# Gated linear attention with a gated convolution layer: the first chunks' convolution in turned 32x32 diagonal blocks on TensorE, and a new order

## The chip, the cores and the metric

One Trainium2 chip, one of its eight cores. The engines of the core work side by side, each through its own queue in order: TensorE (PE) multiplies matrices, VectorE (DVE) and ScalarE (ACT) work element by element, GpSimd (POOL) too, and SyncE (SP) issues the transfers between HBM and the chip's memory, SBUF. TensorE writes its results to PSUM, eight banks of 512 float32 columns on 128 partitions. The metric is the time of one execution in microseconds (us); lower is better.

## The reference

Four sequences of 768 steps, eight heads of 48. The first part is a recurrence with a decayed state, the second a causal convolution of five taps per channel, which gates a projection.

```
f = 1 / (1 + exp(-f_logit))
for t in range(S):                                   # S = 768
    state = f[t] (row by row) * state + outer(k[t], v[t])
    y[t] = q[t] @ state
x = y with the heads side by side                    # [4, 768, 384]
gate_pre[t] = sum over j in 0..4 of conv_w[j] * x[t - 4 + j]
gate = 1 / (1 + exp(-gate_pre))
out = (gate * (x @ w_val)) @ w_out
```

## The kernel before

The 768 steps are six chunks of 128 (c), each with four sequences (b); a sequence's eight heads lie in pairs (p), 48 rows each, on partitions 0 to 47 and 64 to 111. For a chunk, ScalarE forms -log f in two passes (`pexp`, `pln`), VectorE adds it up along time (`scan`), and ScalarE turns the sums into two factors (`exp1`, `exp2`) with which VectorE multiplies q and k (`pmulq`, `pmulk`). TensorE then computes `scores` = k q for a sequence into `aps`, VectorE masks them with a triangle (`mask`, one instruction of 128x1024 into `asb`, one of two buffers); TensorE transposes k (`ktrans` into `kps`, evacuated by `kevac`), applies scores and state to v and q (`apply`, into one of two `xps`, four column tiles of 32 side by side), and forms the chunk's part of the state (`dstate` into `dps`). `stadd` (VectorE) and `stmul` (POOL, line 355) bring the state up to date, `stcopy` (ScalarE) lays it out for the next chunk. `xevac` (ScalarE) copies the result of `apply` into `xf`, channels on partitions: 384 channels are three blocks m of 128; `halo` (POOL, line 328) copies the last four columns of a chunk ahead of the next.

The second layer works on a whole chunk, 512 columns (four sequences by 128 steps); the last chunk is cut into two halves, called 5 and 6. `msplit` (ScalarE) and `mlow` (VectorE) split x into two parts of fewer bits, `xH` and `xL`. The convolution is `mlast` on ScalarE (the newest tap, a multiplication) and four `mconv` on VectorE for each block m, `gt` = `xf` shifted times a weight per partition, plus `gt`; `gate` is the sigmoid. `mval` is a product of nine matmuls (three blocks, three pairs of parts), `mmul` multiplies it by the gate, `mhigh` and `mrest` split the result, and `mout` is nine matmuls more; `mstore` copies to SBUF and sends. The weights come as 64-bit numbers; `weight` (lines 211 to 243) turns them into float32 in eight steps, of which POOL does the first and the last, ScalarE two, VectorE four.

What an engine does and in what order stands in `PROGRAM`, a list of pieces such as `mconv 1 0 2` (chunk 1, block 0, tap 2). `Ordered` binds the instructions of PE, VectorE and ScalarE to that order; POOL and SP take theirs as the scheduler sets it. Tiles in PSUM are fixed: `aps` (two banks), two `xps`, `kps`, `dps` and two `mps` for the projections. `busy` issues matmuls on zeros (26 in the first 18 us). A copy of the computation for extreme inputs (`general`) stands behind a branch and isn't taken here.

Of the kernel before, what the change touches and what calls it, by code (L numbers as in the profile page):

```python
# [37 lines left out]
loadk 1 0; pmulk 0 0; pexp 0 2; loadq 1 0; pmulq 0 0; ktrans 0 0; loadv 0 2; scan 0 1; pln 0 2; scores 0 0; exp2 0 1;  # L40
scan 0 2; wload 1; exp1 0 1; busy 4; kevac 0 0; pmulq 0 1; exp2 0 2; dstate 0 0; pmulk 0 1; busy 4; exp1 0 2;
mask 0 0; loadv 1 0; ktrans 0 1; loadf 2 0; okc 0; kevac 0 1; pmulq 0 2; scores 0 1; pexp 1 0; weight 0; pmulk 0 2;
apply 0 0; pln 1 0; mask 0 1; loadf 3 0; loadk 2 0; dstate 0 1; wload 2; ktrans 0 2; scores 0 2; kevac 0 2; scan 1 0;
xevac 0 0; stadd 0 0; exp2 1 0; ktrans 0 3; mask 0 2; apply 0 1; kevac 0 3; pmulk 1 0; scores 0 3; stcopy 0 0;
scan 1 1; xevac 0 1; exp1 1 0; ktrans 1 0; loadk 2 1; mask 0 3; apply 0 2; exp2 1 1; loadq 2 0; pmulq 1 0; exp1 1 1;
apply 0 3; loadv 2 0; weight 1; weight 0; xevac 0 2; weight 0; pmulq 1 1; scores 1 0; xevac 0 3; weight 1; halo 1;
msplit 0; weight 1; loadq 2 1; weight 1; dstate 0 2; mask 1 0; dstate 0 3; kevac 1 0; ktrans 1 1; weight 0; stadd 0 1;
scores 1 1; kevac 1 1; pmulk 1 1; loadv 2 1; pexp 2 0; weight 0; weight 1; dstate 1 1; weight 1; apply 1 0; okc 1;
mask 1 1; weight 1; loadf 4 0; pln 2 0; weight 1; mlow 0; weight 3; ktrans 1 2; loadk 3 0; scores 1 2; xevac 1 0;
stcopy 0 1; scan 2 0; apply 1 1; mask 1 2; exp2 2 0; exp1 2 0; weight 0; scan 2 1; weight 2; scores 1 3; loadq 3 0;  # L50
mlast 0 0; pmulk 2 0; xevac 1 1; weight 2; exp2 2 1; mconv 0 0 0; dstate 1 0; mask 1 3; apply 1 2; loadv 3 0;
kevac 1 2; exp1 2 1; pmulq 2 0; ktrans 1 3; pmulq 2 1; scores 2 0; loadk 3 1; kevac 1 3; xevac 1 2; mconv 0 0 1;
weight 3; mlast 0 1; stadd 1 0; ktrans 2 0; weight 2; mlast 0 2; dstate 1 2; stmul 1 0; weight 3; dstate 1 3;
weight 3; stcopy 1 0; apply 1 3; weight 2; mask 2 0; kevac 2 0; stadd 1 1; okc 2; scores 2 1; loadv 3 1; weight 2;
xevac 1 3; stmul 1 1; pmulk 2 1; loadq 3 1; stcopy 1 1; mconv 0 2 0; ktrans 2 1; pexp 3 0; dstate 2 0; loadk 4 0;
weight 2; apply 2 0; weight 3; mask 2 1; kevac 2 1; loadf 5 0; weight 2; mconv 0 1 0; pln 3 0; dstate 2 1; weight 2;
mconv 0 1 1; ktrans 2 2; apply 2 1; weight 4; mconv 0 1 2; kevac 2 2; stadd 2 0; weight 3; stmul 2 0; mconv 0 0 2;
weight 3; dstate 2 2; loadq 4 0; stcopy 2 0; scan 3 0; weight 3; scores 2 2; loadv 4 0; weight 5; mconv 0 0 3;
exp2 3 0; mval 0 0; mconv 0 1 3; gate 0 0; mconv 0 2 1; mconv 0 2 2; mval 0 1; mask 2 2; exp1 3 0; mmul 0 0;
ktrans 2 3; scan 3 1; mval 0 2; weight 4; weight 4; exp2 3 1; mconv 0 2 3; exp1 3 1; scores 2 3; pmulq 3 0; halo 2;  # L60
xevac 2 0; pmulk 3 0; kevac 2 3; gate 0 2; apply 2 2; loadk 4 1; mask 2 3; pmulq 3 1; xevac 2 1; dstate 2 3; weight 5;
gate 0 1; scores 3 0; weight 5; xevac 2 2; stadd 2 1; weight 5; stmul 2 1; weight 4; ktrans 3 0; weight 4; apply 2 3;
pexp 4 0; mask 3 0; weight 4; pmulk 3 1; scores 3 1; loadv 4 1; loadq 4 1; mmul 0 1; kevac 3 0; mmul 0 2; weight 4;
ktrans 3 1; pln 4 0; weight 5; weight 4; dstate 3 0; loadk 5 0; weight 5; apply 3 0; mask 3 1; weight 6; weight 5;
scan 4 0; weight 5; weight 6; scores 3 2; kevac 3 1; weight 6; xevac 2 3; exp2 4 0; weight 6; weight 6; apply 3 1;
exp1 4 0; weight 6; mask 3 2; mhigh 0 1; mhigh 0 0; mrest 0 1; dstate 3 1; loadq 5 0; weight 6; mrest 0 0; scores 3 3;
mhigh 0 2; loadv 5 0; weight 6; mlast 1 0; mrest 0 2; mlast 1 1; pmulk 4 0; mout 0 1; msplit 1; mconv 1 0 0;
mconv 1 0 1; mlast 1 2; mout 0 0; mconv 1 1 0; mstore 0 1; mconv 1 0 2; mconv 1 1 1; mout 0 2; mstore 0 0; mlow 1;
ktrans 3 2; mconv 1 0 3; mval 1 0; kevac 3 2; mconv 1 1 2; mstore 0 2; mconv 1 2 0; gate 1 0; stadd 3 0; ktrans 3 3;
mconv 1 1 3; stmul 3 0; mval 1 2; loadk 5 1; mconv 1 2 1; gate 1 1; mmul 1 0; stcopy 3 0; mconv 1 2 2; mval 1 1;  # L70
mhigh 1 0; mconv 1 2 3; kevac 3 3; stcopy 2 1; scan 4 1; halo 3; xevac 3 0; dstate 3 3; xevac 3 1; pmulq 4 0;
dstate 3 2; gate 1 2; apply 3 2; exp2 4 1; stadd 3 1; okc 3; mask 3 3; stmul 3 1; ktrans 4 0; mmul 1 2; pexp 5 0;
scores 4 0; mrest 1 0; mmul 1 1; pmulk 4 1; apply 3 3; mhigh 1 1; mhigh 1 2; mask 4 0; kevac 4 0; exp1 4 1;
dstate 4 0; mrest 1 1; loadq 5 1; mlast 2 0; scores 4 1; loadv 5 1; mrest 1 2; stcopy 3 1; mconv 2 0 0; pln 5 0;
mconv 2 0 1; mout 1 1; mask 4 1; msplit 2; scan 5 1; ktrans 4 1; mout 1 2; xevac 3 2; pmulq 4 1; exp2 5 1; mlow 2;
exp1 5 1; scores 4 2; kevac 4 1; mstore 1 1; pmulq 5 1; mlast 2 2; ktrans 4 2; mout 1 0; kevac 4 2; mconv 2 2 0;
mlast 2 1; mconv 2 0 2; xevac 3 3; scan 5 0; apply 4 0; mconv 2 0 3; exp2 5 0; mconv 2 1 0; exp1 5 0; dstate 4 1;
mconv 2 1 1; apply 4 1; gate 2 0; mask 4 2; pmulk 5 1; mstore 1 0; scores 4 3; mconv 2 2 1; mconv 2 2 2; mval 2 0;
mask 4 3; mstore 1 2; mconv 2 1 2; mval 2 1; mconv 2 2 3; mmul 2 0; pmulq 5 0; mhigh 2 0; ktrans 4 3; mval 2 2;
pmulk 5 0; kevac 4 3; gate 2 2; okc 4; stadd 4 0; scores 5 0; stmul 4 0; msplit 3; mmul 2 2; mconv 2 1 3; mrest 2 0;  # L80
mhigh 2 2; halo 4; dstate 4 2; xevac 4 0; dstate 4 3; mrest 2 2; stcopy 4 0; apply 4 2; stadd 4 1; xevac 4 1;
stmul 4 1; gate 2 1; mlast 3 2; mmul 2 1; apply 4 3; xevac 4 2; mask 5 0; mlast 3 0; mconv 3 0 0; apply 5 0;
mconv 3 0 1; xevac 4 3; mhigh 2 1; mconv 3 0 2; stcopy 4 1; mlow 3; scores 5 1; okc 5; mrest 2 1; mval 3 1; mlast 3 1;
mask 5 1; mconv 3 0 3; mval 3 0; mconv 3 2 0; gate 3 0; mconv 3 2 1; mconv 3 2 2; scores 5 2; mmul 3 0; mconv 3 2 3;
mval 3 2; mask 5 2; mconv 3 1 0; scores 5 3; msplit 4; mconv 3 1 1; mconv 3 1 2; gate 3 2; apply 5 1; mconv 3 1 3;
mmul 3 2; gate 3 1; halo 5; mmul 3 1; mout 2 0; xevac 5 1; mask 5 3; xevac 5 0; mlast 5 2; mlow 4; msplit 5; mout 2 2;
mlast 5 1; mstore 2 0; mlast 5 0; mconv 5 1 0; mlow 5; mout 2 1; mconv 5 0 0; mconv 5 0 1; mconv 5 2 0; mconv 5 0 2;
apply 5 3; mconv 5 1 1; mhigh 3 1; mconv 5 2 1; mhigh 3 2; mhigh 3 0; mrest 3 2; mconv 5 0 3; apply 5 2; mlast 4 2;
mrest 3 1; mstore 2 1; mconv 5 2 2; xevac 5 3; mrest 3 0; mconv 5 1 2; mlast 4 0; mval 4 0; mconv 5 1 3; mconv 4 0 0;
gate 5 1; xevac 5 2; mconv 4 0 1; mstore 2 2; mval 5 0; mlast 6 1; mconv 4 0 2; mlast 6 2; msplit 6; mout 3 0;  # L90
# [561 lines left out]
```

## Time and profile before

| | |
|---|---|
| time, median of 3 runs | 218.72 us (218.57 to 218.86) |
| the profiled execution | 220.51 us, its span 218.8 us |
| PE busy, share of the span | 184.7 us, 84% |
| VectorE | 192.4 us, 88% |
| ScalarE | 144.3 us, 66% |
| POOL | 34.0 us, 16% |
| mean granted clock of TensorE | 0.921 |
| moved by DMA | 31.9 MB |

The span runs from the first to the last instruction. Matmuls are pipelined, so PE's busy time holds time in which one of them drains while nothing else can start. Granted clock: 1 is 2.4 GHz, 0.5 is 1.2 GHz. An instruction's duration overlaps the next one's start on VectorE by some 0.08 us. An engine that is idle costs nothing by itself; what counts is which engine the others wait for, stretch by stretch.

### The profile page before, as it was taken

What the parts mean: (1) busy time and instruction counts of PE and PEld (TensorE: products, weight loads), DVE (VectorE), ACT (ScalarE), POOL (GpSimd) and SP (SyncE); (2) the same over time, 40 slices, a digit from 0 to 9 for tenths busy, and PEclk for the clock granted to TensorE, in tenths of its full rate; (3) what the DMA queues carried; (4) which work ended last, traced back from release to release, by engine and by line L of the source; (5) the groups of instructions that cost most, each with busy time, mean ns of one, the idle gap of its engine ahead of it and who ended that gap; (6) DMA issues with size and microseconds to landing.
All of it is one profiled execution on the core that took longest, in us unless ns stands there. A gap on an engine that the chain in (4) does not pass through costs nothing.

```text
span 218.8 us, 5685 instructions
## 1 busy us (share of the span) xinstructions
PE 184.7 (84%) x2438; PEld 148.4 (68%) x2438; DVE 192.4 (88%) x251; ACT 144.3 (66%) x226; POOL 34.0 (16%) x37
## 2 busy tenths in 40 slices
PE   7599599857997478768999888999989999999970
PEld 2257468755876366557787767877868788889870
DVE  5396998999999999999979999999799999997700
ACT  5767678777492989768289988737823769453530
POOL 4001001500437522312035000002100000000000
PEclk9959958988699999995899996999999999999996
DMA  6999999964079021722141321020000102210231
GB/s 165 368 414 425 414 419 421 415 231 163 23 269 325 36 69 39 271 85 98 61 132 50 100 82 48 3 99 3 3 3 0 36 15 99 96 48 27 96 145 38
DMA packets 10976, 31.91 MB, mean 146 GB/s; under 512 B 1344, under 2 KB 2368, under 8 KB 10688
## 3 DMA queue, kind: packets, MB, share of 16 engines
q1 hardware_dynamic: 10944, 31.48, 38.7%
q8 instruction: 21, 0.34, 0.6%
q14 instruction: 11, 0.09, 0.1%
HBM read 26.75 MB, written 4.72 MB: 144 GB/s over the span
## 4 chain that ended last, share of the span: by engine, by line
DVE 41%; PE 33%; ACT 11%; issue 5%; DMA 5%; SPq 1%; DVEq 0%; ACTq 0%
PE mps L113 21%; DVE gt L113 10%; DVE e L113 10%; DVE asb L113 7%; ACT e L113 5%; PE aps L113 5%; DMA kb<-in_k 5%; PE xps L113 3%; DVE kb L113 3%; DVE qb L113 3%; DVE ca L113 2%; PE kps L113 2%; DVE cb L113 2%; PE dps L113 2%; DVE xL L113 2%
## 5 line engine op out<-in xcount | busy, mean ns | idle before, releaser
L113 ACT ACTIVATE e<-e 112x1024 f32<-112x1024 f32 (+3 forms) x40 | 40.0, 1004 | 18.1 <-DVE e L113 17.7
L113 DVE SCALAR_TENSOR_TENSOR gt<-xf,cws,gt 128x512 f32<-128x512 f32 x60 | 45.4, 775 | 0.6
L113 PE MATMUL aps<-qb,kb 48*128 48x128 f32 x384 | 30.4, 302 | 13.0 <-DVE asb L113 10.7
L113 PE MATMUL xps<-asb,vb 128*32 128x128 f32 x768 | 38.3, 295 | 0.9 <-DVE asb L113 0.9
L113 PEld LDWEIGHTS aps<-qb,kb 48*128 48x128 f32 x384 | 25.6, 204 | 18.8 <-DVE asb L113 12.8
L113 PEld LDWEIGHTS xps<-asb,vb 128*32 128x32 f32 x768 | 32.8, 118 | 2.4 <-ACT e L113 0.9
L113 PE MATMUL mps<-rg,woH 128*128 128x512 f32 (+1 forms) x102 | 33.5, 414 | 0.3 <-DVE gt L113 0.3
L113 PE MATMUL xps<-qb,st 112*32 112x128 f32 x480 | 31.5, 286 | 1.8 <-ACT xf L113 1.8
L113 DVE TENSOR_TENSOR_SCAN e<-keep,e 112x1024 f32<-112x1024 bf16 (+1 forms) x13 | 29.1, 2247 | 3.1 <-ACT e L113 3.0
L113 DVE TENSOR_TENSOR asb<-aps,tri 128x1024 f32<-128x1024 f32 x24 | 29.1, 1214 | 0.2 <-PE aps L113 0.2
L113 PEld LDWEIGHTS xps<-qb,st 112*32 112x32 f32 x480 | 22.5, 114 | 4.1 <-ACT xf L113 2.1
L113 PEld LDWEIGHTS mps<-rg,woH 128*128 128x128 f32 x102 | 19.8, 206 | 4.7 <-DVE gt L113 0.6
L113 PE MATMUL mps<-xH,wvH 128*128 128x512 f32 x45 | 18.6, 414 | 3.1 <-DVE gt L113 2.9
L113 PE MATMUL mps<-rg,woL 128*128 128x512 f32 (+1 forms) x51 | 20.6, 404 | 0.0
L355 POOL TENSOR_TENSOR ss<-u,e 112x384 f32<-112x384 f32 x8 | 9.4, 1173 | 61.7 <-DVE u L113 57.8
L113 PE MATMUL mps<-xL,wvH 128*128 128x512 f32 x45 | 17.9, 397 | 0.9 <-DVE xL L113 0.9
L113 DVE TENSOR_TENSOR kb<-kb,e 112x1024 f32<-112x1024 f32 (+1 forms) x13 | 15.4, 1185 | 3.5 <-DMA kb<-in_k 3.5
L113 PE MATMUL mps<-xH,wvL 128*128 128x512 f32 x45 | 17.8, 395 | 0.0
L113 PE MATMUL kps<-ident,kb 112*128 112x112 f32 x80 | 13.3, 295 | 3.4 <-DVE kb L113 2.3
L113 DVE TENSOR_TENSOR qb<-qb,e 112x1024 f32<-112x1024 f32 (+1 forms) x13 | 14.6, 1130 | 0.0
L113 ACT COPY osb<-mps 128x512 f32<-128x512 f32 x15 | 8.6, 584 | 8.8 <-PE mps L113 6.5
L113 ACT CAST rg<-gt 128x512 fp32r<-128x512 f32 x15 | 9.0, 616 | 8.1 <-DVE gt L113 5.5
(107 smaller groups left out, 308.5 us busy)
## 6 DMA issues: line engine op xcount, KB each, us to landing
...
```

The source lines that it names most:

```text
L113: ins = emit(*a, **kw)
L355: nc.gpsimd.tensor_tensor(out=ss[:, HS[h]], in0=U[h][:], in1=decay(c, h), op=ALU.mult)
```

## The change

**Convolution of chunks 0 and 1.** For these chunks `mlast` and `mconv` are replaced by `pconv`. The five weights of a channel stand on the diagonals of 32x32 blocks (`diag`, formed once by VectorE from `cws` and `eye`), and one tap is twelve float32 matmuls of 32 rows, 32 columns of weights and 512 moving columns: row group i and block m write to partitions 32 x ((i + m) mod 4) of the bank of m. So the twelve use twelve different tiles of the array, and in a group of 32 partitions the three blocks write three different banks; but block m comes out turned by 32 x m partitions. The gate is read from PSUM by `gate`. Since the gate is turned, the projection must be too: `wv` comes with 480 columns instead of 384 in a row block, from which `mval` takes turned columns, and `mout` uses copies of `wo` with turned rows (`woHr`, `woLr`), made by eight transfers on SP (`wturn`). Chunks 2 to 6 keep `mlast` and `mconv`.

**POOL** sets constants only. `stmul` and the last step of the weights (`wlow`) go to VectorE, `halo` to ScalarE; the first step of the weights is another one (`wabs` on ScalarE, a limit on VectorE in `wbits`).

**PSUM** is one tile, `bank`, of eight banks, and each piece is given a bank by the number behind it in `PROGRAM`. Scores take any two neighbours.

**Order.** `PROGRAM` is a new list, SP is bound to it as well, copies and transfers of the output are two pieces (`ocopy`, `ostore`), and `busy` is not in it. f is turned into the decay in place (`fb` instead of `e`), chunk 0 goes in four parts of 512 columns, `keep` is float32, and the test for extreme inputs is made of three pieces at the end.

```
-    def mgate(w, m):
-        act(SIG, w["gt"][:, m], w["gt"][:, m], AF.Sigmoid)
...
+    def pconv(w, j, zs):
+
+        for i in range(4):
+            for m in range(NM):
+                r, o = slice(32 * i, 32 * i + 32), 32 * ((i + m) % 4)
+                PE.matmul(bank[o : o + 32, zs[m], : w["n"]], diag[r, m * KT + j], w["xf"][r, m, w["b"], j : j + C],
+                          start=(j == 0), stop=(j == HALO), tile_position=(32 * i, o))
+
+    def mgate(w, m, z):
+        g = w["gt"][:, m]
+        act(SIG, g, g if z is None else bank[:, z, : w["n"]].rearrange("p (b t) -> p b t", t=C), AF.Sigmoid)
...
+    def wturn(m):
+
+        for s, d in ((woH, woHr), (woL, woLr)):
+            for to, of in ((slice(32 * m, 128), slice(0, 128 - 32 * m)), (slice(0, 32 * m), slice(128 - 32 * m, 128))):
+                SP.dma_start(d[to, m - 1].bitcast(F32), s[of, m].bitcast(F32))
+
+    def wdiag():
+        DVE.tensor_tensor(out=diag[:], in0=cws[:].unsqueeze(2).to_broadcast([128, NM * KT, 32]),
+                          in1=eye[:].unsqueeze(1).to_broadcast([128, NM * KT, 32]), op=ALU.mult)
...
+    def wbits(n):
+        ca, cb = wab(n)
+        hi, bi = wdst(n)[:, :, 1], cb.bitcast(I32)
+        DVE.tensor_scalar(out=cb, in0=cb, scalar1=low, scalar2=big, op0=ALU.max, op1=ALU.min)
+        DVE.tensor_scalar(out=bi, in0=bi, scalar1=3, scalar2=0x3FFFFFF8, op0=ALU.logical_shift_left, op1=ALU.bitwise_and)
+        DVE.scalar_tensor_tensor(out=bi, in0=hi, scalar=-(1 << 30), in1=bi, op0=ALU.bitwise_and, op1=ALU.bitwise_or)
+        x = cws[:] if n == 0 else ca
+        DVE.scalar_tensor_tensor(out=x.bitcast(I32), in0=wdst(n)[:, :, 0], scalar=29, in1=bi,
+                                 op0=ALU.logical_shift_right, op1=ALU.bitwise_or)
...
     def stmul(c, h):
-        nc.gpsimd.tensor_tensor(out=ss[:, HS[h]], in0=U[h][:], in1=decay(c, h), op=ALU.mult)
+        DVE.tensor_tensor(out=ss[:, HS[h]], in0=U[h][:], in1=decay(c, h), op=ALU.mult)
...
+    def mval(w, m, po):
+        at = WCOLS[m] + (0 if w["turn"] else 32 * m)
+        mm3(po, lambda kk: wvH[:, kk, at : at + 128], lambda kk: wvL[:, kk, at : at + 128], w["xH"], w["xL"])
...
+        def of(t, tr):
+            return lambda kk: (tr[:, kk - 1, cols] if w["turn"] and kk else t[:, kk, cols])
```

How the order moves, at three places. PE in chunk 1, before: scores (`aps`), transposition (`kps`) and state parts (`dps`) of chunk 1 stand behind the state parts of chunk 0, and `apply` (`xps`) follows.

```order
L113 MATMUL aps<-qb_65,kb_67 128x128 x8
L113 MATMUL dps<-vb_70,ksb_86 48x48 x8
L113 MATMUL dps<-vb_70,ksb_87 48x48 x8
L113 MATMUL kps<-ident,kb_67 128x112 x4
L113 MATMUL aps<-qb_65,kb_67 128x128 x8
L113 MATMUL dps<-vb_71,ksb_87 48x48 x8
L113 MATMUL xps_105<-qb_65,st 32x128 x4
```

The same place now; all results go to `bank`.

```order
L126 MATMUL bank<-ident,kb_67 128x112 x8
L126 MATMUL bank<-xf_88,diag 32x512 x12
L126 MATMUL bank<-qb_65,kb_67 128x128 x16
L126 MATMUL bank<-xf_88,diag 32x512 x48
L126 MATMUL bank<-vb_71,ksb_86 64x48
```

The first tap of chunk 0's convolution comes ahead of two sequences' scores, the other four, 48 matmuls, ahead of the first state part of chunk 1.

VectorE around the second half of chunk 2's scans, before: masks (`asb`), convolution of chunk 0 (`gt<-xf,cws,gt`), weights (`ca`, `cb`), state (`u`).

```order
L113 TENSOR_TENSOR asb_85<-aps,tri 128x1024
L113 SCALAR_TENSOR_TENSOR gt<-xf_90,cws,gt 128x512 x3
L113 TENSOR_TENSOR u_88<-ss,dps 112x384
L113 SCALAR_TENSOR_TENSOR ca_102<-raww_95,cb_103 128x384
L113 SCALAR_TENSOR_TENSOR gt<-xf_90,cws,gt 128x512
L113 SCALAR_TENSOR_TENSOR e_82<-keep,e_82 112x1024
L113 SCALAR_TENSOR_TENSOR gt<-xf_90,cws,gt 128x512 x4
L113 TENSOR_TENSOR asb_84<-aps,tri 128x1024
```

Now, behind the masks of chunk 1 (the two rows with `fb_68` twice are the scans of chunk 2, `gt<-bank,gt` is `mmul` of chunk 0):

```order
L126 TENSOR_TENSOR u_77<-ss,bank 112x384
L126 TENSOR_TENSOR asb_85<-bank,tri 128x1024
L126 TENSOR_TENSOR ss<-u_77,fb_69 112x384
L126 TENSOR_TENSOR asb_84<-bank,tri 128x1024
L126 TENSOR_TENSOR gt<-bank,gt 128x512
L126 SCALAR_TENSOR_TENSOR fb_68<-keep,fb_68 112x1024 x2
```

The convolution steps are gone here, the product with the gate follows the masks at once, and `stmul` stands as `ss<-u,fb` in VectorE's own queue.

VectorE at the start, before: the first scan (`e<-keep,e`) is the first work after the constants.

```order
L113 MEMSET dps 32x384
L113 SCALAR_TENSOR_TENSOR e_81<-keep,e_81 112x512
L113 TENSOR_TENSOR kb_66<-kb_66,e_83 112x512
L113 TENSOR_TENSOR qb_64<-qb_64,e_81 112x512
L113 SCALAR_TENSOR_TENSOR e_81<-keep,e_81 112x512
```

Now (`cws` the convolution's weights, `raw_97` the first block of `wv`):

```order
L126 SCALAR_TENSOR_TENSOR cws<-rawcw,cb_99 128x15
L126 TENSOR_TENSOR diag<-cws,eye 128x480
L126 TENSOR_SCALAR cb_101<-cb_101 128x480 x2
L126 SCALAR_TENSOR_TENSOR cb_101<-raw_97,cb_101 128x480
L126 SCALAR_TENSOR_TENSOR ca_100<-raw_97,cb_101 128x480
L126 SCALAR_TENSOR_TENSOR fb_68<-keep,fb_68 112x512 x2
L126 TENSOR_TENSOR kb_66<-kb_66,e_72 112x512
```

`diag` and one block of weights stand ahead of the first scan.

## Rows read from the trace of the kernel before

**Rows 1.** Busy time by stretch: bounds, length, each engine's busy us, clock, DMA, GB/s

```profile
0.00:15.35 15.35, 11.76 (x46) 5.47 (x48) 9.51 (x14) 9.80 (x16) 2.51 (x11) 0.84 0.88 309
15.35:171.37 156.02, 132.18 (x2069) 107.65 (x2068) 149.30 (x174) 111.03 (x161) 31.52 (x26) 0.92 0.41 153
171.37:218.80 47.43, 40.79 (x329) 35.31 (x327) 33.58 (x67) 23.48 (x50) 0.00 (x0) 0.96 0.19 69
```

**Rows 2.** Timeline of VectorE: start, duration; a product, the first and the last mask

```profile
10.24 0.69 DVE L113 TENSOR_TENSOR qb<-qb,e 112x512 f32<-112x512 f32 x1
...
15.35 1.23 DVE L113 TENSOR_TENSOR asb<-aps,tri 128x1024 f32<-128x1024 f32 x1
...
171.37 1.21 DVE L113 TENSOR_TENSOR asb<-aps,tri 128x1024 f32<-128x1024 f32 x1
```

**Rows 3.** Waits: who for whom, us in total, times, longest

```profile
PE aps L113 <- DVE asb L113: 10.7, 7, 2.8
...
DVE kb L113 <- DMA kb<-in_k: 3.5, 1, 3.5
```

**Rows 4.** Chain of waits in order of time: start, us, what (records counted)

```profile
170.72 6.56 PE mps L113 x27
177.28 3.21 PE xps L113 x112
...
183.85 2.09 PE mps L113 x9
...
209.92 1.06 PE aps L113 x9
...
212.08 0.37 ACT fb L113
```

**Rows 5.** Groups by line and shape: count, busy us, mean ns, idle before

```profile
L113 DVE SCALAR_TENSOR_TENSOR gt<-xf,cws,gt 128x512 f32<-128x512 f32 x60 | 45.4, 775 | 0.6
...
L113 DVE TENSOR_TENSOR_SCAN e<-keep,e 112x1024 f32<-112x1024 bf16 x11 | 26.8, 2433 | 2.2 <-ACT e L113 2.0
...
L113 DVE TENSOR_TENSOR u<-ss,dps 112x384 f32<-112x384 f32 x8 | 4.4, 544 | 0.0
...
L113 DVE SCALAR_TENSOR_TENSOR cb<-ca,cb 128x384 int32<-128x384 int32 x6 | 4.1, 690 | 0.1
...
L113 DVE SCALAR_TENSOR_TENSOR ca<-raww,cb 128x384 int32<-128x384 int32 x6 | 3.6, 597 | 0.1
...
L113 DVE SCALAR_TENSOR_TENSOR ca<-cb,ca 128x384 f32<-128x384 f32 x6 | 3.2, 543 | 0.6 <-ACT cb L113 0.6
...
L113 DVE TENSOR_SCALAR cb<-ca 128x384 int32<-128x384 int32 x6 | 2.5, 443 | 0.1
```

**Rows 6.** Tiles `gt` and `e`: shortest, median, longest ns, first and last start

```profile
L113 DVE SCALAR_TENSOR_TENSOR gt<-xf,cws,gt x60: 721/750/1395, 49.2 to 195.2; 128x512 f32<-128x512 f32 x60
...
L113 DVE TENSOR_TENSOR_SCAN e<-keep,e x13: 1221/2284/3107, 4.9 to 135.8; 112x1024 f32<-112x1024 bf16 x11, 112x512 f32<-112x512 bf16 x2
```

**Rows 7.** Timelines of POOL and VectorE, from 66 to 69 us

```profile
66.89 1.09 POOL L355 TENSOR_TENSOR ss<-u,e 112x384 f32<-112x384 f32 x1 [1.10 <-DVE u L113]
...
67.20 1.33 DVE L113 SCALAR_TENSOR_TENSOR gt<-xf,cws,gt 128x512 f32<-128x512 f32 x1
```

**Rows 8.** Timeline and chain of PE: one `apply` of chunk 0; `dstate`, `ktrans`, `scores`

```profile
19.01 1.08 PE L113 MATMUL xps<-asb,vb 128*32 128x128 f32 x32
...
34.59 0.52 PE dps L113 x16
...
35.66 0.60 PE kps L113 x4
36.26 1.12 PE aps L113 x16
```

**Rows 9.** Timeline of POOL: setting the state to zero, and a small copy

```profile
1.13 1.38 POOL L197 MEMSET st<- 112x1536 f32 x1
...
33.38 0.22 POOL L328 COPY xf<-xf 128x48 f32<-128x48 f32 x1 [7.31 <-ACT xf L113]
```

More of the change, by code (lines that the diff above doesn't have):

```diff
@@ L7 @@
 from concourse import mybir
-from concourse.masks import make_identity
 from concourse._compat import with_exitstack
@@ L41 @@
[L41 to L90, printed above, removed]
@@ new lines @@
+scan 1 1; loadq 1 1; wbits 3; msplit 0; exp2 1 1; okc 0; loadf 2 0; loadv 1 1; loadq 2 0; scores 1 1 @6;
+scores 1 0 @0; pconv 0 1 @3 4 5; pconv 0 2 @3 4 5; pconv 0 3 @3 4 5; pconv 0 4 @3 4 5; dstate 1 0 @2; mask 1 1 @6;
+pmulk 1 1; mask 1 0 @0; loadf 2 1; ktrans 1 2 @6; exp1 1 1; whigh 3; stcopy 0 0; apply 1 0 @7; dstate 1 1 @2;
+wbits 2; pmulq 1 1; gate 0 0 @3; gate 0 1 @4; kevac 1 2 @6; stcopy 0 1; apply 1 1 @3; whigh 2; xevac 1 0 @7;
+gate 0 2 @5; wlow 2; mlow 0; wlow 3; dstate 1 2 @0; stadd 1 0 @2; halo 1; pexp 2 0; scores 1 3 @4; scores 1 2 @6;
@@ new lines @@
+stmul 2 1; scan 3 0; gate 1 0 @5; gate 1 1 @6; mask 2 3 @0; loadv 3 0; loadk 3 0; mval 1 0 @5; mval 1 2 @6;
+mval 1 1 @0; whigh 5; gate 1 2 @7; wbits 6; exp2 3 0; exp1 3 0; pmulk 3 0; whigh 6; wlow 6; wlow 5; mask 2 2 @2;
+mmul 1 2 @6; ktrans 3 0 @1; apply 2 3 @7; loadf 4 1; loadf 4 0; pmulq 3 0; pexp 4 0; pln 4 0; xevac 2 3 @7;
+apply 2 2 @2; xevac 2 2 @2; scores 3 0 @6; scores 3 1 @2; xevac 2 1 @4; kevac 3 0 @1; dstate 3 0 @1; scan 3 1;
+ktrans 3 1 @4; exp2 3 1; halo 3; msplit 2; stcopy 2 1; exp1 3 1; kevac 3 1 @4; mask 3 0 @6; loadk 3 1; wturn 1;
@@ new lines @@
+pexp 5 0; stcopy 3 1; pln 5 0; mconv 2 0 2; mconv 2 1 1; mconv 2 2 0; mconv 2 0 3; loadv 4 1; ocopy 1 1 @7 1;
+gate 2 0; mconv 2 1 2; mconv 2 2 1; mconv 2 1 3; mconv 2 2 2; scan 5 1; mmul 2 0 @2; mconv 2 2 3; gate 2 1;
+kevac 4 1 @3; kevac 4 0 @0; mhigh 2 0; ocopy 1 0 @4 2; msplit 3; gate 2 2; scores 4 3 @6; scores 4 2 @2;
+ostore 1 2 @0; ostore 1 1 @1; mmul 2 1 @5; scan 5 0; mlow 3; dstate 4 0 @0; apply 4 1 @5; apply 4 0 @4; xevac 4 1 @5;
+mhigh 2 1; xevac 4 0 @4; mmul 2 2 @1; mrest 2 1; mlast 3 1; mhigh 2 2; mrest 2 0; mask 4 2 @2; dstate 4 1 @0;
@@ new lines @@
+apply 4 2 @3; gate 3 2; mmul 3 2 @6; ocopy 2 1 @7 1; kevac 4 3 @4; mconv 3 0 2; mmul 3 1 @5; mconv 3 0 3;
+xevac 4 3 @2; dstate 4 3 @0; xevac 4 2 @3; halo 5; gate 3 0; halo 4; mhigh 3 2; msplit 4; scores 5 0 @6; mask 5 0 @6;
+scores 5 1 @2; scores 5 3 @4; scores 5 2 @6; mask 5 1 @2; mrest 3 2; stadd 4 1 @0; mmul 3 0 @1; apply 5 0 @2;
+apply 5 1 @3; stmul 4 1; mlast 4 2; mhigh 3 1; stcopy 4 1; mhigh 3 0; mask 5 2 @6; apply 5 2 @0; xevac 5 2 @0;
+xevac 5 0 @2; mconv 4 2 0; mask 5 3 @4; mrest 3 1; mrest 3 0; mlow 4; mlast 4 1; mlast 4 0; mconv 4 0 0; okc 4;
```

625 lines of the change are left out of this document (317 added, 308 removed).

## The prediction

> **What bounds the kernel now.** Four views, in this order. First the table of busy time by stretch [rows 1], cut at the first and the last `mask` on VectorE [rows 2]: these are pieces that both programs have in the same number (24), so they serve as milestones. In the long middle stretch VectorE is busy for 149.3 of 156.0 us, and no other engine comes near without a qualification: PE shows 132.2 us, but at a mean clock of 0.92, and ScalarE 111.0. So from 15 to 171 us VectorE is the bound, and loses only 6.7 us. Second the waits [rows 3]: PE waits longest for VectorE's masks (10.7 us), because there is one scores tile, `aps`. VectorE itself has one wait of size for a load, 3.5 us, and that is in the head. Third the end of the chain of waits [rows 4]: from 170.7 us it stays on PE, through 41 us of matmuls back to back, until one last copy at 212.1; the span ends at 218.8, 6.7 us later. So the tail (47.4 us) is PE's: VectorE is busy for 33.6 us of it. Fourth the prices [rows 5 to 9].
>
> The profiled execution took 220.51 us, 1.7 more than its span and 0.8% above the median of 218.72. I build a span and scale it by 218.72/220.51.
>
> **Prices on PE, at the full clock** [rows 4, 8]. The trace counts each float32 matmul as two records. A batch's scores cost 1.12, a transposition group 0.60, `dstate` 0.52, `apply` 1.6 (two take 3.21; in chunk 0, without the state's part, 1.08), a projection group of nine 2.09, one of half width 1.06.
>
> **Convolution on PE.** No row shows it. Twelve float32 matmuls make one tap, each on its own 32x32 tile with 512 columns. Nearest row: two `apply`s are 112 records of 128 columns on four column tiles, so 28 steps in 3.21 us, 0.115 each, with four different streams side by side into one bank. Four times the columns and two records make 0.92 us for a tap if all twelve tiles run side by side: 4.6 us for a chunk, 9.2 for both. The other bound is 12 x 0.92 = 11 us for a tap if none do. In between lies the case that tiles of different rows of the array exclude each other: four times 0.92, 18.3 us for a chunk. I take 9.2: each of the two kinds of sharing has a row. Column tiles share streams and a bank in `apply`; and 16 score records with 48 rows each take 1.12 us, 0.070 a record, against 0.115 for a record of the same 128 columns in the `apply` lane, so row halves do run side by side there, into two banks.
>
> What speaks against it: in the turned layout, tiles of four different row groups write the same bank at one time, at different partitions, and no row shows that. The Trainium skill forbids it as it stands: TensorEngine Tiling (Array Packing), Restrictions and Gotchas, says that different row tiles can't access the same PSUM bank simultaneously. By it the tap would cost four times as much; this is rival B below. Another page of the Trainium skill, TensorE: Matmul & The Clock Gate, Part 3, gives 10.6 times for sixteen tiles, two thirds of the ideal; with two thirds here a chunk would cost 6.9 instead of 4.6 us, and the forecast would be some 4 us higher (an estimate from that page; no run here shows it).
>
> **VectorE, part by part.** The middle stretch holds 149.3 us of busy time; its instructions change so:
> - Convolution of chunks 0 and 1: 24 of 84 steps go. 23 fewer stand in the middle stretch (25 instead of 48): 23 x 0.775 = -17.8 [rows 5].
> - `stmul` comes from POOL: 8 multiplications like `u` at 0.54: +4.3.
> - Weights: six blocks of 384 columns cost 4.1 + 3.6 + 3.2 + 2.5 = 13.4 [rows 5], the small one some 0.7: 14.1. Now three blocks of 384 and two of 480 stand in the middle (one of 480 is in the head), each with two clamping or shifting steps and two merging ones: 2 x 0.443 + 0.690 + 0.597 = 2.17 for 384, a quarter more, 2.72, for 480; and six subtractions that POOL did, at `u`'s 0.54 and 0.68. Together 6.5 + 5.4 + 3.7 = 15.6: +1.5.
> - POOL works no longer beside VectorE. At 67.2 us a convolution step took 1.33 us while POOL multiplied [rows 7]; the median is 0.75, the longest 1.40, and scans of 1024 have a median of 2.28 and a longest of 3.11 [rows 6]. What means lie above medians is 11 x 0.15 for the scans and 36 x 0.025 for the steps that stay, 2.5 us; merging steps, `kb`, `xL` and `mrest` are stretched in the same places, and I take 5.5 for all, with 2.5 and 7 as ends: -5.5.
> - One more `mrest`, chunk 0 in finer parts: +1.1. The scan's `keep` is float32 instead of bfloat16: no row shows that. A product of 512 float32 with two inputs takes 0.69, a scan of 512 takes 1.22 [rows 2, 6], so reading isn't what limits the scan; I take 0, at most +0.3 each (3 us).
>
> Sum: 149.3 - 17.8 + 4.3 + 1.5 - 5.5 + 1.1 = 133 us.
>
> **PE in the same stretch.** The new program puts there 22 scores (24.6), 19 transpositions (11.4), 20 `dstate` (10.4), 4 + 19 `apply` (4.3 + 30.4), 21 projection groups (43.9) and ten taps (9.2): 134 us. The same sum for before is 120 us, shown as 132.2 busy at the clock of 0.92. So PE gains 14 us and draws level with VectorE; ScalarE stays near 107 (6 `mlast` go, five halo copies and wider `kevac` come). **The middle stretch** can't be under 134. If PE loses only the 6.7 us that VectorE loses now, it is 141; if its work is stretched as before (132.2/120 = 1.10), 148. Scores have any two of eight banks now, so the 10.7 us of waits for masks can largely go; but two full engines that feed each other lose more than one. I take 145.
>
> **Head.** Now the first mask starts at 15.35. In the new order VectorE must first multiply `diag` from POOL's `eye`, with the first weight block and all scans queued behind. POOL starts at 0.8 and sets `keep`, both `ksb` and `st` at the rate of the 1.38 us for 1536 columns [rows 9]: 0.9 + 0.8 + 1.4, and small ones, taken as 1.5: 5.4. Four copies of `eye` take 0.22 each (nearest row) or up to 0.9: 6.3 to 8.8; I take 6.5. Then `diag` and the block (0.6 + 2.0), four scans of 512 (1.22 each) and four products (0.69) [rows 2, 6]: 16.7. Range 15.4 to 19. The 26 warm-up matmuls of `busy` go: PE waits for keys until then, and they cost nothing but the two groups of four between pieces of chunk 0.
>
> **Tail.** After the last mask PE has one `apply`, 9 full and 12 half projection groups: 1.6 + 18.8 + 12.7 = 33.1; before it was two, 11 and 12: 38.9 of 47.4 us. The remainder, 8.5, stays: 41.6. VectorE's 29 us there, plus the last three half groups (3.2), the copy and 6.4 us to the end, make 39; so PE bounds, and I add 0.9 for the two crossing: 42.5, at most 46.
>
> **Loads.** An eighth more weight data and eight copies that turn `wo`'s halves: DMA is busy for 0.41 of the middle stretch, that hides them. f is now decayed in place, so its next load waits for the end of the chunk before last; a chunk of some 25 us covers it. Nothing is charged; were loads late as in the head, 3.5 us each.
>
> **Sum.** 16.7 + 145 + 42.5 = 204.2 us of span; (204.2 + 1.7) x 0.9919 = 204.2 us. With the lower ends 15.4 + 141 + 41.6 = 198, with the upper 19 + 149 + 46 = 214.
>
> **Rivals.**
> - **A, the forecast:** 204 (198 to 213), chance 0.70.
> - **B, row tiles exclude each other in a bank.** Place: the taps of `pconv`. Each costs 3.7 instead of 0.92, 13.7 us more a chunk. PE keeps its order: behind the taps of chunk 0 stand `dstate`, transpositions and `apply` of chunk 1, behind those of chunk 1 the same of chunk 2; masks and evacuations wait with them. PE and VectorE are level there, so nearly all comes through: 204 + 26 = 230. It ends slower than before from 2.4 us a tap (15 us over ten). For it: no row with four row groups in one bank. Against it: the four land on different partitions, as `apply`'s four do. Chance 0.11.
> - **C, PE takes the bound, and the lower clock stays.** Without `busy` and with a dense stream from many banks PE starts low; if its 134 us are stretched by 1.10 and VectorE's 6.7 us of waits come on top, the middle is 155 and the time 214. For it: 0.92 in the middle stretch, where PE waits for masks; against it: these waits are what the new banks take away. Chance 0.12.
> - **D, better:** under 198, with both engines hardly waiting in spite of being level. Chance 0.05.
> - **E, the tiles don't run side by side at all:** 11 us a tap, ten of them 110 instead of 9: about 305. The rates of `apply` and scores speak against it. Chance 0.02.
>
> **How the numbers follow.** The likeliest is A: 204. Below 198 lie 0.05; B and E, 0.13, lie above 217; so 198 to 217 leaves out 0.18. Runs of this kernel differ by 0.13%, so about 0.2% can be told from no change. Faster: A, D and nearly all of C, 0.86; within 0.2%: the upper edge of C, 0.01; slower: B and E, 0.13.
>
> **What would show it.** Right: a group of 240 records into `bank` from `diag` with about 9 us in union, ten taps near 0.9; VectorE near 173 us in all (192.4 now), scans with a mean near 2.3 and none over 3; POOL silent after 9 us; first mask near 17, last near 162; the chain ends with PE, 33 us after it. Wrong: taps over 2 us; or PE and VectorE both well under 85% between the masks, with waits of each for the other; or a last mask near 170 in spite of a VectorE sum of 133.

## The result and the profile after

The changed kernel takes **200.7 us** (median of four runs, 198.26 to 203.34) where the kernel before takes 218.8 beside it: a ratio of 0.907, with a 95% interval of 0.896 to 0.918. The forecast was 204.0, with 198 to 217 as its range. Runs of one kernel differ with the granted clock (the changed kernel's span is 196.6 us at a mean clock of 0.998 and 201.6 at 0.973), so ratios here and below compare the fast runs of two kernels on the same chip (of these four the 198.26 and 199.52; the medians alone would give 0.917), and the profiles of `unturned` (251.5 us) and `unturned_m` (213.7), which fell in slow runs, are used below for the durations of single pieces and for shares.

The profiled execution took 199.52 us, its span is 197.8. Busy time by stretch, cut again at the first and last `mask`, answers to [rows 1] (columns as there):

```profile
0.00:16.46 16.46, 3.06 (x20) 2.45 (x20) 11.82 (x18) 12.79 (x25) 5.08 (x20) 1.00 0.88 310
16.46:157.04 140.58, 136.75 (x2351) 112.45 (x2355) 131.92 (x157) 110.47 (x163) 0.00 (x0) 0.99 0.50 181
157.04:197.80 40.76, 34.48 (x291) 30.21 (x281) 31.27 (x65) 19.78 (x45) 0.00 (x0) 0.96 0.17 60
```

The middle stretch is 15.4 us shorter than before, the tail 6.7 shorter, the head 1.1 longer. In the middle VectorE (third busy column) falls from 149.3 to 131.9 us, and PE (first) stands at 136.8 of 140.6 us, at a clock of 0.99 instead of 0.92.

The waits, beside [rows 3] (who for whom, us in total, times, longest):

```profile
PE bank L126 <- DVE kb L126: 12.6, 1, 12.6
...
DVE asb L126 <- PE bank L126: 2.1, 5, 0.8
```

PE's first wait is the head, when there are no keys yet. Its 10.7 us of waits for masks are gone; now VectorE waits for scores, 2.1 us in all. The end of the chain, beside [rows 4]:

```profile
149.95 41.46 PE bank L126 x475
...
191.48 0.37 ACT osb L126
```

One unbroken run of PE up to the last copy, as before, but it ends 34.4 us after the last mask instead of 40.7. Last, the convolution on PE (timeline: start, us, records) and its group (busy us, mean ns), and VectorE's scans and steps, beside [rows 5]:

```profile
30.34 1.11 PE L126 MATMUL bank<-xf,diag 32*32 32x512 f32 x24
31.39 2.06 PE L126 MATMUL bank<-qb,kb 48*128 48x128 f32 x32
33.37 4.08 PE L126 MATMUL bank<-xf,diag 32*32 32x512 f32 x96
```

```profile
L126 PE MATMUL bank<-xf,diag 32*32 32x512 f32 x240 | 10.8, 597 | 0.0
```

```profile
L126 DVE SCALAR_TENSOR_TENSOR gt<-xf,cws,gt 128x512 f32<-128x512 f32 x36 | 25.3, 746 | 0.0
L126 DVE TENSOR_TENSOR_SCAN fb<-keep,fb 112x1024 f32<-112x1024 f32 x10 | 22.8, 2284 | 1.7 <-ACT fb L126 1.7
```

A tap is 24 records: from 30.34 to the next piece at 31.39 it is 1.05 us; ten of them make 10.8. The 24 missing steps and work that is no longer stretched (scans of 2284 ns instead of 2433) are most of what VectorE saves.

### The profile page after: what moved, and what is told of

Same layout as the page of the kernel before. It is cut to its first block, busy times and chain, and to the rows that moved or that the text cites. A ratio compares the mean times of both kernels' runs of the same rounds, so it can differ in the third digit from the quotient of the medians.

```text
span 197.8 us, 6124 instructions
## 1 busy us (share of the span) xinstructions
PE 174.3 (88%) x2652; PEld 145.1 (73%) x2652; DVE 175.0 (88%) x238; ACT 143.0 (72%) x231; POOL 5.1 (3%) x20
## 4 chain that ended last, share of the span: by engine, by line
PE 76%; ACT 7%; DMA 6%; DVE 5%; issue 2%; SPq 0%; ACTq 0%; DVEq 0%
PE bank L126 76%; DMA fb<-in_f 4%; ACT fb L126 3%; DMA raw<-in_wv 3%; ACT e L126 1%; DVE asb L126 1%; DVE gL L126 1%; DVE cb L126 1%; ACT L126 1%; DVE fb L126 1%; DVE qb L126 1%; DVE ss L126 1%; DVE u L126 0%; ACT st L126 0%; ACT osb L126 0%
## 5 line engine op out<-in xcount | busy, mean ns | idle before, releaser
L126 ACT ACTIVATE fb<-fb 112x512 f32<-112x512 f32 (+2 forms) x32 | 36.7, 1162 | 4.2 <-DMA fb<-in_f 3.8
L126 PE MATMUL bank<-asb,vb 128*32 128x128 f32 x768 | 37.0, 286 | 0.8 <-issue 0.8
L126 PEld LDWEIGHTS bank<-asb,vb 128*32 128x32 f32 x768 | 31.9, 115 | 1.9 <-issue 1.3
L126 DVE TENSOR_TENSOR asb<-bank,tri 128x1024 f32<-128x1024 f32 x24 | 29.1, 1221 | 3.6 <-PE bank L126 2.1
L126 PE MATMUL bank<-qb,st 112*32 112x128 f32 x480 | 31.0, 282 | 0.0
L126 PE MATMUL bank<-qb,kb 48*128 48x128 f32 x384 | 27.7, 292 | 3.8 <-DVE gt L126 1.5
L126 PEld LDWEIGHTS bank<-qb,kb 48*128 48x128 f32 x384 | 24.6, 199 | 7.0 <-issue 1.9
L126 DVE TENSOR_TENSOR_SCAN fb<-keep,fb 112x1024 f32<-112x1024 f32 (+1 forms) x14 | 27.5, 1978 | 1.7 <-ACT fb L126 1.7
L126 DVE SCALAR_TENSOR_TENSOR gt<-xf,cws,gt 128x512 f32<-128x512 f32 x36 | 25.3, 746 | 0.0
L126 PEld LDWEIGHTS bank<-qb,st 112*32 112x32 f32 x480 | 22.6, 113 | 2.0 <-ACT ksb L126 0.8
L126 PE MATMUL bank<-ident,kb 112*128 112x112 f32 x80 | 11.2, 272 | 12.6 <-DVE kb L126 12.6
L126 PEld LDWEIGHTS bank<-ident,kb 112*128 112x128 f32 x80 | 8.6, 144 | 16.5 <-issue 12.8
L126 ACT COPY xf<-bank 128x384 f32<-128x384 f32 x24 | 10.9, 476 | 10.7 <-PE bank L126 10.7
L126 ACT COPY osb<-bank 128x512 f32<-128x512 f32 (+1 forms) x21 | 10.7, 520 | 8.4 <-PE bank L126 8.1
L126 PEld LDWEIGHTS bank<-vb,ksb 128*64 128x64 f32 (+1 forms) x320 | 10.7, 130 | 4.5 <-issue 2.4
```

Of the source, the lines that this page charges most:

```text
L126: ins = emit(*a, **kw)
```

## The experiments

The question is what made the 15.4 us in the middle and the 6.7 in the tail: VectorE's relief (theory 1), the new order with its banks (theory 2), or both together (theory 3, formed after the first two had been tried). Ratios are to the kernel before, on the same chip; the changed kernel's own, run again, stands first.

**The changed kernel again.** 

> The changed kernel once more, on the chip of the next three runs, as their yardstick. Both theories: 198 to 203 us, with the span between the first and the last mask near 140 us and PE busy in over 95% of it.

Measured: 199.55 us, ratio 0.908 (0.895 to 0.920). This is the base below.

**The convolution back on VectorE, in the new order.**

```
-CONV_PE = (0, 1)
+CONV_PE = ()
-pconv 0 0..4, pconv 1 0..4; gate c m @z
+mlast 0 m; mconv 0 m j; ... mrest 0 0; mlast 1 m; mconv 1 m j; gate c m
```

(`PROGRAM` shortened; `wdiag` and `wturn`, which nothing needs then, are left out too.)

> The changed kernel's order and bank numbers, with the convolution of chunks 0 and 1 back on VectorE (24 steps, none on PE; chunk 1's steps stand behind chunk 0's last `mrest`). Theory 1 (VectorE's relief is the gain): VectorE's middle stretch grows from 131.9 by 23 x 0.775 = 17.8 to about 150, no engine can end it sooner, and the time is 213 to 218. Theory 2 (the new order and the banks dealt by piece are the gain, wherever the convolution stands): at most 204. In between, 205 to 212, both carry a part.

Measured: 212.7 us, ratio 0.978 (0.968 to 0.989). Its stretches (middle and tail):

```profile
16.70:173.20 156.50, 133.35 (x2110) 113.97 (x2114) 147.68 (x181) 114.80 (x169) 0.00 (x0) 0.92 0.43 157
173.20:211.70 38.50, 34.48 (x291) 30.22 (x282) 31.26 (x65) 19.74 (x45) 0.00 (x0) 0.99 0.18 63
```

Just under theory 1's range, far from theory 2's. The rows say more than the time does: with VectorE at 147.7 us the middle stretch is 156.5, no shorter than before (156.0), so the new order gives nothing there by itself. But the tail is 38.5 instead of 47.4 us: **the tail's gain is the order's**, with no help from the convolution. Most of it is a shift: PE is busy for 34.5 us behind the last mask instead of 40.8, and what went stands in the middle stretch now. (A first version, with chunk 1's steps so early that they overwrite a tile that chunk 0 still needs, took 215.0 us.)

**One chunk of the two on PE.**

```
-CONV_PE = (0, 1)
+CONV_PE = (0,)
```

> The changed kernel with chunk 0's convolution on PE and chunk 1's on VectorE. VectorE's middle stretch is then 131.9 + 12 x 0.775 = 141, PE's 136.7 - 4.9 = 132. Theory 1 with a maximum (the fuller of PE and VectorE sets the middle stretch, plus some 4 us of waits): middle 145, time 203 to 206. Theory 1 with a sum (two nearly full engines lose in proportion to VectorE's work): half of the way between 199.6 and 215, so 206 to 209. Theory 2 (order and banks): 198 to 202.

Measured: 205.1 us (204.2 to 210.5), ratio 0.940 (0.929 to 0.951). The profiled execution took 207.1:

```profile
16.10:165.40 149.30, 137.45 (x2233) 115.22 (x2237) 139.63 (x170) 112.73 (x166) 0.00 (x0) 0.95 0.48 171
```

VectorE's busy time came out as summed (139.6 for 141). The place of the convolution matters (theory 2's 198 to 202 is out), step by step: none, one, two chunks on PE give 0.978, 0.940, 0.908. Between the maximum and the sum of theory 1 the runs don't decide, since they lie on the border. PE's busy time hardly moves along these three profiles (133.4, 137.5, 136.8 us), though the taps add 10.8 us: the granted clock of the middle stretch goes from 0.92 over 0.95 to 0.99. How much of the gain comes by that clock was not tried apart.

**The relief alone, in the old order.**

```
-mconv 0 m j; ... mconv 1 m j        (24 pieces of the kernel before)
```

> The kernel before, with its own order and banks, without the 24 convolution steps of chunks 0 and 1 on VectorE (left out: the gates of these chunks use the newest tap alone). Theory 1 (VectorE's relief is the gain): its middle stretch falls from 149.3 to about 131 us of VectorE's work, and the time to 201 to 207. Theory 2 (order and banks carry it): PE's waits for masks of the one scores tile stay, and the time is 212 or more. Between: PE's 132 us at the low clock bound the stretch, about 208 to 211.

Measured: 214.8 us (211.8 to 215.9), with 218.4 (216.2 to 221.3) for the kernel before. Middle stretch, two waits, and three places behind the second of them:

```profile
15.70:164.90 149.20, 127.80 (x2053) 104.40 (x2052) 131.08 (x150) 110.56 (x161) 30.09 (x26) 0.94 0.43 160
```

```profile
PE aps L115 <- DVE asb L115: 11.3, 8, 2.9
...
DVE gt L115 <- ACT gt L115: 11.9, 4, 6.4
```

```profile
65.07 1.05 ACT L115 COPY st<-ss 48x384 f32<-48x384 f32 x2 [2.23 <-POOL ss L357]
...
69.18 0.69 DVE L115 TENSOR_TENSOR gt<-mps,gt 128x512 f32<-128x512 f32 x1 [3.66 <-ACT gt L115]
...
105.22 0.69 DVE L115 TENSOR_TENSOR gt<-mps,gt 128x512 f32<-128x512 f32 x1 [6.40 <-ACT gt L115]
```

**Theory 1 falls here.** VectorE lost 18.2 us of work and the stretch only 6.8 (the time, by the medians, 3.6); VectorE is now idle for 18 us in it, and PE waits for masks as long as before (11.3 us for 10.7). What is new is the other wait: VectorE waits 11.9 us for ScalarE's gates, where the kernel before shows

```profile
DVE gt L113 <- ACT gt L113: 2.8, 2, 1.6
```

Up to the eleventh mask (64.32 us, 74.38 before) the relief came through, 10.1 us of it. Then VectorE, whose next piece is the product with the gate, stands still for 3.7 us and later for 6.4: the gate's place in ScalarE's queue is behind copies that wait for POOL's state product (65.07) and for PE. By these rows it is mainly the old order of the other engines that keeps the relief back; this run doesn't show the one scores tile to be the cause, and no run took POOL's work and the convolution steps out of the old kernel together. Neither half of the change does it: relief without the order gives 6.8 us of the middle, order without relief nothing, both 15.4.

**One batch's scores at a time, in the new kernel.** Of the order, this takes back one thing.

```
-scores 0 1 @0; exp1 0 3; pexp 1 0; mask 0 0 @2;
+exp1 0 3; pexp 1 0; mask 0 0 @2; scores 0 1 @0;      (and eleven more)
```

> The changed kernel with one batch's scores at a time: twelve of the 24 `scores` pieces are moved behind the `mask` of the batch before them, as one scores tile in two banks would force it; banks and everything else stay. Theory 3 (a second pair of banks for the scores is what lets the relief of VectorE through): PE's waits for masks come back, some 10 us as in the kernel before, and the time is 206 to 211. Rival (the order of the rest or the relief alone is enough): at most 202.

Measured: 204.6 us (204.4 to 204.8), ratio 0.933 (0.926 to 0.941).

```profile
16.40:161.30 144.90, 137.24 (x2337) 111.27 (x2337) 131.94 (x157) 110.82 (x164) 0.00 (x0) 1.00 0.49 176
```

```profile
DVE asb L129 <- PE bank L129: 7.2, 8, 2.0
...
PE bank L129 <- DVE asb L129: 2.4, 4, 1.0
```

Between the two expectations: 5 us of the time, 4.3 of the middle stretch. Theory 3 is right that the scores' banks matter, but the wait sits mostly on the other engine: VectorE waits for scores 7.2 us instead of 2.1, PE for masks only 2.4. So a second pair of banks is worth a quarter of the middle's gain, or a little more; the larger rest of the order's part (where gates and evacuations stand) was not tried piece by piece.

**PE's share of the price.** In this run eight of the ten taps are left out.

```
-        for i in range(4):
+        for i in range(4 if j == HALO else 0):
-                          start=(j == 0), stop=(j == HALO), ...
+                          start=True, stop=True, ...
```

> The changed kernel with one tap of five in each of `pconv`'s two chunks (left out: the other eight taps, so the gates of these chunks use the newest tap alone). PE's middle stretch loses eight taps of 1.0 us and goes to 128.7 us of work, VectorE's stays at 131.9. If PE sets the stretch now, the 8 us come through: 190 to 193. If VectorE does, nearly nothing: 197 to 200. With both at nearly the same load, a part: 193 to 197.

Measured: 196.1 us (194.7 to 197.3), ratio 0.892 (0.883 to 0.902), some 3 us less than with the taps.

```profile
16.40:154.90 138.50, 131.62 (x2158) 111.89 (x2162) 131.86 (x157) 110.72 (x163) 0.00 (x0) 0.96 0.51 184
```

PE has 8.4 us of taps less, the stretch is only 2.1 shorter. The time lies in the third range, that of two engines at the same load. The rows are less clean than that: the clock of this stretch is 0.96 instead of 0.99, so PE's busy time fell by 5.1 us only, and VectorE, at 131.9 us as before, is idle for 6.6.

**What turning the blocks is for.** In the turned form the block of rows 32 i and output group m stands at column group (i + m) mod 4, so twelve blocks lie on twelve tiles of the array. Unturned, the three groups m of one i share a tile.

```
-                r, o = slice(32 * i, 32 * i + 32), 32 * ((i + m) % 4)
+                r, o = slice(32 * i, 32 * i + 32), 32 * i
```

(With it the projection goes back to unturned weights, and `wturn` is left out.)

> The changed kernel with the 32x32 blocks on the array's diagonal, not turned: the three output groups of a tap then share one tile of the array each, so that only four of the twelve run side by side (the turned copies of the output weights go with it). A tap goes from 1.0 to 2.6 to 3.0 us, ten taps add 16 to 20 us to PE. If PE now sets the middle stretch (136.7 busy of 140.5 us), all of it comes through: 215 to 220. If PE has room there and VectorE sets it (131.9), some 12 us or less come through: 204 to 212. If tiles of different row groups excluded each other in a bank, nothing would change against the turned form: 199 to 202, with taps as long as now.

Measured: 232.1 us, ratio 1.065 (1.055 to 1.075), beyond all three expectations. One tap:

```profile
30.37 5.42 PE L129 MATMUL bank<-xf,diag 32*32 32x512 f32 x24
```

5.4 us, twice the 2.6 to 3.0 that I had expected for four blocks side by side. I divided it by 24, took the 0.226 us for one record alone, and concluded that nothing ran side by side; that is wrong, as the start times below show. In the program's order (i outside, m inside) neighbours on PE's queue share a tile. Hence a second run with the loops exchanged:

```
-        for i in range(4):
-            for m in range(NM):
+        for m in range(NM):
+            for i in range(4):
```

> The kernel `unturned`, with the two loops of a tap exchanged: the four blocks of one output group stand one behind the other, so that neighbours on PE's queue lie on different tiles of the array's diagonal. In `unturned` neighbours shared a tile, and a tap took 5.4 us, 0.226 us a record, with nothing side by side. Theory Q (the queue runs in order, so a matmul that must wait for its own tile holds all behind it): four now run side by side, a tap takes three times 0.45 us and a little more, 1.4 to 1.8, and the time is 203 to 208. Theory D (blocks on the diagonal don't run side by side, in whatever order): the tap stays at 5.4, the time at 230 to 234.

Measured: 209.3 us, ratio 0.954 (0.946 to 0.962).

```profile
33.01 2.78 PE L129 MATMUL bank<-xf,diag 32*32 32x512 f32 x24
```

```profile
L129 PE MATMUL bank<-xf,diag 32*32 32x512 f32 x240 | 27.2, 590 | 0.0
```

```profile
16.30:173.60 157.30, 155.57 (x2353) 118.29 (x2357) 132.05 (x158) 110.94 (x163) 0.00 (x0) 0.99 0.43 157
```

The order on the queue halves the tap (33.01 to 35.72: 2.7 us), so theory D falls; theory Q has the sign, but not the size, for 1.4 to 1.8 was expected. The start times of the records settle the sizes. These are the records under way in the first 0.44 us of a tap, in the changed kernel, in `unturned_m` and in `unturned`:

```profile
30.34 0.69 PE L126 MATMUL bank<-xf,diag 32*32 32x512 f32 x12
...
33.01 0.63 PE L129 MATMUL bank<-xf,diag 32*32 32x512 f32 x4
...
30.37 0.61 PE L129 MATMUL bank<-xf,diag 32*32 32x512 f32 x1
```

The twelve start within 0.07 us, the four within 0.02; the next ones start 0.45 us later, and after that the steps are 0.43 us apart (in the four taps in a row each twelve fall into five and seven, at the same pace). So a step takes the same time with one record, four or twelve in it, and a tap's 24 records take two steps on twelve tiles, six with four tiles in turn, and twelve in `unturned`. There one to three records start at a step (1, 1, 2, 2, 3, 3, 3, 3, 2, 2, 1, 1), which fits four tiles that each take their six records one behind another and begin two steps after one another. With nothing side by side it would be 24 steps, 10.3 us. Theory Q's 1.4 to 1.8 went by the 0.226 us; with two records of 0.43 us a matmul, three in a row make 2.6. The stretch shows the other side of the balance: PE is busy for 155.6 of 157.3 us, and VectorE has 25 us to spare. By the ratios, 16 us more of taps (27.2 for 10.8 in all) cost 10 us here, and 43 more (5.4 for 1.05 a tap) cost 34 in `unturned`: what is added to PE comes through for the most part.

**POOL's work.** First in the new kernel, the state's multiplication and the weights' subtraction go back to POOL:

```
-        DVE.tensor_tensor(out=ss[:, HS[h]], in0=U[h][:], in1=decay(c, h), op=ALU.mult)
+        nc.gpsimd.tensor_tensor(out=ss[:, HS[h]], in0=U[h][:], in1=decay(c, h), op=ALU.mult)
```

> The changed kernel with stmul (8 multiplications) and wlow (6 subtractions) on POOL again, all else as changed. Theory 1 (PE is the bound now, VectorE has some 8 us to spare between the masks): VectorE's busy time falls by 4 us net (8 less work, 3 to 5 more from stretching beside POOL), the time stays within 1.5 us of the changed kernel. Rival (POOL's stretching of VectorE's work was a main part of the old loss): scans and steps stretched to 3.0 and 1.3 us come back, and the time rises by 4 us or more.

Measured: 202.6 us, ratio 0.925 (0.913 to 0.936). Middle stretch; then POOL's products and VectorE's `kb` (shortest, median, longest ns):

```profile
16.20:159.90 143.70, 138.68 (x2348) 113.60 (x2352) 127.77 (x143) 110.20 (x163) 21.72 (x14) 0.99 0.50 178
```

```profile
L390 POOL TENSOR_TENSOR ss<-u,fb x8: 842/850/4926, 46.3 to 157.4; 112x384 f32<-112x384 f32 x8
...
L126 DVE TENSOR_TENSOR kb<-kb,e x14: 666/1216/1906, 11.5 to 149.3; 112x1024 f32<-112x1024 f32 x10, 112x512 f32<-112x512 f32 x4
```

VectorE has 4 us less to do and the time is some 3 us longer, though the intervals overlap, so the sign is likely, not shown. That lies between the two expectations, and the rival's cause didn't come: scans have a mean of 2281 ns and convolution steps of 745, as without POOL. Much of the loss falls in one place: chunk 4's load of f stands behind POOL's products here and starts at 112.19 us instead of 108.67, and its scan at 124.24 instead of 121.07. Second, the same work taken from POOL in the kernel before:

```
-            nc.gpsimd.tensor_tensor(out=dst[1], in0=x, in1=dst[0].bitcast(F32), op=ALU.subtract)
+            DVE.tensor_tensor(out=dst[1], in0=x, in1=dst[0].bitcast(F32), op=ALU.subtract)
```

> The kernel before, with the state's multiplication and the weights' clamping and subtraction on VectorE instead of POOL. VectorE gets 8 x 0.54 + 6 x 0.54 and some 2 us of clamping, near 9.5 us, and loses what POOL stretched: 5.5 us by the prediction (2.5 to 7). By the prediction's term: 220 to 226. If POOL's share of VectorE's time was underrated, and waits for POOL's results cost as well: 213 to 218.

Measured: 217.6 us, ratio 1.000 (0.996 to 1.004).

```profile
15.30:167.80 152.50, 127.70 (x2053) 103.79 (x2051) 150.30 (x195) 111.11 (x162) 6.80 (x5) 0.94 0.42 157
```

```profile
L113 DVE SCALAR_TENSOR_TENSOR gt<-xf,cws,gt 128x512 f32<-128x512 f32 x60 | 43.7, 745 | 0.6
...
L113 DVE TENSOR_TENSOR_SCAN e<-keep,e 112x1024 f32<-112x1024 bf16 x11 | 25.1, 2282 | 0.8 <-ACT e L113 0.7
```

Twenty-one more instructions, and VectorE's busy time in the middle rises by 1.0 us (150.3 for 149.3). Beside [rows 5] the sixty steps fall from 45.4 to 43.7 us and the scans from 26.8 to 25.1. The ratio says no change: the time lies in the second range, near its upper edge, and the first, which went by the prediction's term, is too high. So this part of the change is neutral by itself.

**The head in another order.** Keys, queries and f are loaded before the large weight block, `diag` and that block come behind chunk 0's first mask. (In it a weight load comes before the block ahead of it has been read, which changes values, but no instruction is missing.)

```
-wload 0; wabs 0; wbits 0; wdiag; loadf 0 0; wload 1; ... wbits 1; ... scan 0 0;
+loadf 0 0; wload 0; pexp 0 0; ... wbits 0; scan 0 0; ... mask 0 0 @2; ... wdiag; ... wbits 1;
```

> The changed kernel with another order of chunk 0: keys and queries of the first four pairs are loaded ahead of the first block of weights, and diag and the first block of weights follow the scans instead of standing ahead of them. The pieces are the same. Theory 1 (PE bounds from its first scores on): PE's first matmul comes at 9.5-10.5 instead of 12.6 us and the time falls by 1.5 to 3 us. Rival (the middle stretch is paced by VectorE and by loads): the early start is lost again in chunk 1, the time is within 0.7 us.

Measured: 201.5 us, ratio 0.916 (0.903 to 0.928): no gain, and 1.9 us longer than the base; neither expectation had that. The chain to the first mask (start, us, what), and below it that of the changed kernel:

```profile
3.64 5.70 DMA fb<-in_f
...
9.35 6.38 DMA qb<-in_q
...
16.56 1.21 DVE asb L129
```

```profile
1.74 5.02 DMA raw<-in_wv
...
9.59 1.23 DVE fb L126
```

The first mask comes at 16.56 us, as in the changed kernel (16.46), though `diag` and the weight block now come later. Here the loads of f and q set it: the scan ahead of the mask on VectorE's queue starts at 15.4 us, released by a load. In the changed kernel it is the load of the weight block, VectorE's work on it, and the scans behind. PE starts earlier in this run (11.3 us for 12.6), but the weight block is now paid behind the third mask, and the fourth comes at 28.0 us instead of 26.5.

## Why the prediction came out

**The sum.** The span was to be 16.7 + 145 + 42.5 = 204.2; it is 16.5 + 140.6 + 40.8 = 197.8. The forecast's 204.0 is 3.3 us above the median, for two terms of the same sign. (The prediction gives 148 us as the upper end of the middle and adds up with 149; nothing hangs on it.) The middle is 0.4 us under its lower end of 141, the tail 0.8 under its own.

**The mis-sized term is what two full engines lose.** VectorE's work was predicted well (133; 131.9), PE's nearly (134; 136.8 busy, of which the taps are 10.8 instead of 9.2). But 11 us were put on PE's 134 for feeding each other; the stretch is 6.6 longer than that, and 3.8 longer than PE's own busy time. The lower end of 141 assumed that PE loses what VectorE lost before, 6.7 us, and that is nearly what came: 6.6, of which 1.6 are the dearer taps. PE's waits for masks are gone from its list; VectorE is idle for 8.7 us.

**Where the prediction was right for a reason that it named only in half.** Its middle stretch took VectorE's relief as what brings the gain, and mentioned the banks as what lets the waits for masks go. `old_noconv` shows that relief needs a condition which the prediction doesn't name: in the old order, where VectorE then waits 11.9 us for ScalarE's gates, 18 us of relief bring 6.8. The banks are the smaller part of it: `one_scores` prices them at 4.3 us of the stretch. And `new_noconv` fits "PE draws level with VectorE": 8 us less on PE bring 2.1 (at a clock of 0.96).

**The tap.** 0.92 us was forecast from `apply`; it is 1.05, near the bound taken and far from 3.7 and 11. Rivals B and E fall: all four row groups write one bank within a tap, at different partitions. If they took turns, the eight records of a bank at the 0.43 us measured from one record on a tile to the next would need 3.4 us; instead all twelve records of a step start within 0.07 us. And E's 11 us a tap was well sized: 24 steps make 10.3. The rule of the Trainium skill (TensorEngine Tiling (Array Packing), Restrictions and Gotchas), that different row tiles can't access the same PSUM bank simultaneously, is not borne out for tiles on different partitions; for tiles on the same partitions no run here shows anything. The two thirds of the Trainium skill's other page (TensorE: Matmul & The Clock Gate, Part 3), an estimate of 6.9 us a chunk, were a little too much: it is 5.4.

**Rival C** (the lower clock stays) did not come: 0.99 in the middle, with PE hardly waiting. In `conv_dve2`, where PE is busy for 133 of 156.5 us, the stretch stands at 0.92, as it did before.

**POOL.** The stretching term was 5.5 us, with 2.5 and 7 as ends. From the groups of the kernel before and of `old_nopool`, steps 1.7 and scans 1.7 show directly, and all groups that stand in both some 7 us: the upper end. (The busy time as a whole agrees: 21 instructions more, 9.7 us by their groups, for 1.0 us, less the 0.08 us by which each overlaps the next.) That is most of the 1.1 us by which VectorE came out under the sum. In the new kernel the scans have a mean of 2284 ns, as forecast.

**The head** came out at 16.46 for 16.7, by a chain whose first link is another one: not POOL's `eye` but the load of the weight block, which lands at 6.8 us, and ScalarE's step on it; `diag` is done before that. The block, the scans and the products behind are as priced. `head` adds that a second path, the loads of f and q, has the same length. So the size was right in part by luck.

**The tail** was to keep the 8.5 us of the 47.4 in which PE did no counted work; with the new order it keeps 7.7 (40.8 - 33.1). The kernel with the convolution on VectorE has 38.5, so the order could have been seen to act here apart from the convolution; the prediction did count the smaller work of PE (33.1 for 38.9), which is most of it.

**Loads.** Nothing was charged for f being decayed in place. One place shows it, in chunk 4's scan (start, us, and in brackets the idle time before):

```profile
121.07 2.29 DVE L126 TENSOR_TENSOR_SCAN fb<-keep,fb 112x1024 f32<-112x1024 f32 x1 [1.74 <-ACT fb L126]
```

The chain behind it is a load of f that was issued only at 108.7 us, when the last product of the old values had been made, and ScalarE's two steps. VectorE loses 1.7 us there; PE has projections in the meantime.
